# Seventeen opening dummy products, values on 120 partitions, a head planned anew, and a last block summed in two column parts

## The chip, the cores and the metric

The kernel runs on one core of one Trainium2 chip. The metric is the device time of one execution in microseconds (us), taken as the median of several executions. A core has a matrix engine (TensorE, "PE" in the profile; "PEld" is its loading of weights), a vector engine (VectorE, "DVE"), a scalar engine (ScalarE, "ACT"), GpSimd ("POOL") and SyncE ("SP"), whose queue starts nearly all transfers from memory here. Each engine takes its instructions strictly in the order in which they were written, and waits for the others through semaphores.

## What is computed

Two batches of 12480 tokens with 128 channels go through an attention over 49 agents and then through a two-layer MLP with 2048 hidden features and a leaky rectifier. All data are 32-bit floats.

```python
scale = 1.0 / np.sqrt(q.shape[-1])
def sm(a, b):                       # softmax over the last axis
    s = scale * (a @ b.transpose(0, 2, 1))
    e = np.exp(s - s.max(-1, keepdims=True))
    return e / (e.sum(-1, keepdims=True) + 1e-09)
agent_v = sm(agents, k) @ v         # (2, 49, 128): over all 12480 tokens
x = sm(q, agents) @ agent_v         # (2, 12480, 128)
h = x.reshape(-1, 128) @ w_in       # (24960, 2048)
out = np.maximum(0.01 * h, h) @ w_out
```

## The kernel before

The program has a head, a body and a tail.

**The head** needs all of batch 0's keys and values, because `agent_v` sums over every token. Keys come in 13 chunks (`load_k`, 480 KB each), values in 13 chunks (`load_v`), weights in 8 pieces (`load_w`; they arrive as 64-bit floats, 512 KB a piece, and are turned into 32-bit floats by hand) and the first queries in `load_q`. The host lays the values out as 120 partitions for each batch; for batch 0 `load_v` joins both batches' partitions and takes the first 128 of them, so that 8 rows of batch 1 come along unused. The loads of the head stand on SP's queue in the order of the string `ORDER` (k, v, w and q, one letter for a load). Keys and values share a ring of `LD = 9` buffers, weights one of `NVR = 4`: a load waits until the one 9 (or 4) places before it in its ring has been used up.

What the engines do with the loads: `k_score` (TensorE, the line `ps[r, j * w:j * w + NA]`, L397 before) gives a chunk's scores. For the first `NW = 4` chunks a weight load covers 120 columns, later ones go as 64 and 56 columns. `k_run` (VectorE, L417) keeps the running maximum, `k_copy` (ScalarE) stores the scores. When all 13 chunks are through, `k_max0` to `k_max3` (from L431 on) reduce the maximum, `k_sub` and `k_exp` make the exponentials, and `k_av32` (L541) sums exponentials times values, chunk after chunk, into one accumulator. Then `f_copy`, `f_tr`, `f_avT` and `m_half` form the folded weights `m_hi` and `m_lo`, with which the body's first product (`mm1`, tile `h`, L825) can start. Meanwhile each weight piece is converted: `conv_bits` (L273, L274), `conv_mant`, `conv_exp`, `conv_low` (L289), `conv_sign` (L296), `conv_mul` (L303), and `wo_hi_of`, `wo_lo_of` (L309) for pieces of `w_out`. The first two blocks of queries run through their softmax in the head too (`chain`).

The order of all this on each engine is made by a small planner, the class `Plan`. It keeps a time at which each engine is free, takes the step that can begin first, and adds to each step's beginning a number of `slack` by which it may be put off (the table `slack`, and `other` for the query chain). A TensorE gap in the plan is filled with dummy products (`heat`, L1015: 128 by 128 from a tile of zeros, each recorded as two matmuls). Ahead of the plan stands `heat(9, True)`, the opening dummy products.

**The body** goes over 52 blocks (`NBLK`) of 480 tokens (`NB`), 8 steps (`NP`) each. A step has six pairs of matmuls for the first layer (`mm1`), the rectifier split into two parts (`relu`: `hi` on ScalarE, `lo` on VectorE), and, two steps later, six pairs for the second layer (`mm2`, L855). Each pair works on both halves of the 128 rows (`ROWS`), 64 rows each, into two PSUM banks; `o_copy` and `o_add` add the two and store the block. The PSUM pairs `turns[0]` and `turns[1]` change roles from block to block: one is the block's output, the other (`aux2`) serves side work.

**The tail** is the last block's `o_copy`: for each half of 240 tokens ScalarE copies one bank (L883), VectorE adds the other (L884), and a transfer stores the half, the first from SP's queue, the second from ScalarE's.

Of the kernel before, what the change touches and what calls it, by code (L numbers as in the profile page):

```python
# [13 lines left out]
ALU = mybir.AluOpType  # L14
# [4 lines left out]
class Plan:  # L19
# [6 lines left out]
    def add(self, name, eng, cost, fn, args, after, lag=80):  # L26
        self.steps[name] = eng, cost, fn, args, after, lag
# [47 lines left out]
def tile_agent_attention_then_leaky_mlp(  # L75
# [27 lines left out]
    nc = tc.nc  # L103
# [3 lines left out]
    P = 128  # L107
    TP = 120
    NJ = N // TP
    G = 4  # L110
    NB = G * TP
    BPB = N // NB
    NBLK = B * BPB
    NF = DFF // P
# [12 lines left out]
    NP = NF // 2  # L127
# [3 lines left out]
    RP = 4  # L131


    ORDER = "kqwkkkwwkkkkwqkkkkkwvwvvvvvvvvvvwvvwq"
    HOP = 90
    WW = slice(2 * C, 3 * C)
    EW = HALF + NA
# [21 lines left out]
    def aux2():  # L159
        return turns[owner[0] % 2]  # L160
# [4 lines left out]
    def halves(i):  # L165

        owner[0] = i
        return [turns[(i + 1) % 2][:, g, :] for g in range(2)]
# [9 lines left out]
    ROWS = slice(0, HALF), slice(HALF, P)  # L178
# [10 lines left out]
    wo_hi = const.tile([P, NF, C], F32R, name="wo_hi")  # L189
    wo_lo = const.tile([P, NF, C], F32R, name="wo_lo")  # L190
# [6 lines left out]
    l_hi = [const.tile([P, C], F32R, name=f"l_hi{b}") for b in range(B)]  # L197
    l_lo = [const.tile([P, C], F32R, name=f"l_lo{b}") for b in range(B)]
# [4 lines left out]
    run = const.tile([TP, CH, NA], F32, name="run")  # L203
# [13 lines left out]
    def load_v(b, c):  # L217

        t = ld.tile([P, CH, C + 2], F32, tag="ld", name="vt")
        j = slice(c * CH, (c + 1) * CH)  # L220
        if b == 0:
            nc.sync.dma_start(out=t, in_=v.rearrange("b p j c -> (b p) j c")[:P, j, :])
        else:
            nc.sync.dma_start(out=t[:TP], in_=v[b, :, j, :])
        v_t[b, c] = t

    def load_q(i):
# [146 lines left out]
    def prep_parts(b):  # L374
        a, t = a_sb[:, b, :], prep_t.pop(b)
        for o, x, n in SLOTS[:2] + ((SL + A0 - 1, A0 - 1, 1),):
            nc.vector.tensor_copy(t[:, o:o + n], a[:, x:x + n])
        nc.vector.tensor_copy(a_hl[b][:, :HALF], t)
        sub(nc.vector, a_hl[b][:, HALF:], t, a_hl[b][:, :HALF].bitcast(F32))
# [277 lines left out]
    qs_t, s_t, x_t, r_t2, pT_t = {}, {}, {}, {}, {}  # L657
# [158 lines left out]
    h_t, r_t, o_t = {}, {}, {}  # L816
# [28 lines left out]
    def mm2(i, p):  # L845

        b = i // BPB
        if p == 0:
            o_t[i] = halves(i)
        o = o_t[i]  # L850
        hi, lo = r_t.pop((i, p))

        def add(w, x, start=False, stop=False):
            for g, r in enumerate(ROWS):
                nc.tensor.matmul(o[g][:, :NB], lhsT=w[r], rhs=x[r], start=start, stop=stop)  # L855

        for g in range(2):
            f = 2 * p + g
            add(wo_hi[:, f, :], hi[:, g], start=(f == 0))
            add(wo_lo[:, f, :], hi[:, g])  # L860
        if p == (NP // 2 if i % BPB else NP - 1):
            t = pT_t[i]
            for w, x, g in ((l_hi, 0, 0), (l_lo, 0, 1), (l_hi, 1, 0)):
                g ^= i % 2 == 0
                r = ROWS[g]
                nc.tensor.matmul(  # L866
                    o[g][:, :NB], lhsT=w[b][r], rhs=t[r, x], start=False, stop=False
                )
        for g in range(2):
            f = 2 * p + g  # L870
            add(wo_hi[:, f, :], lo[:, g], stop=(f == NF - 1))

    def o_copy(i):
        t = p1.tile([P, 2, NB], F32, tag="oT", name="oT")
        o = o_t.pop(i)
        if i < NBLK - 1:
            for g in range(2):
                nc.scalar.copy(t[:, g], o[g][:, :NB])  # L878
            x_t["o"] = t
            return  # L880
        h = NB // 2
        for c, eng in ((slice(0, h), nc.sync), (slice(h, NB), nc.scalar)):
            nc.scalar.copy(t[:, 1, c], o[1][:, c])  # L883
            nc.vector.tensor_tensor(out=t[:, 0, c], in0=o[0][:, c], in1=t[:, 1, c], op=ALU.add)  # L884
            eng.dma_start(out=out[:, i * NB + c.start:i * NB + c.stop], in_=t[:, 0, c])

    def o_add(i):
# [7 lines left out]
    def at(step, fn, *a):  # L895
# [3 lines left out]
    chain = (  # L899
        (-16, q_hi), (-16, q_lo), (-13, q_mm), (-13, q_turn), (-12, q_mm2), (-12, q_x), (-12, q_add),  # L900
        (-11, q_tr), (-10, q_red), (-10, q_swap), (-9, q_mx), (-9, q_sub), (-7, q_exp),
        (-7, q_sum), (-7, q_swap), (-6, q_rec), (-6, q_norm), (-5, p_trans), (-4, p_hi),
        (-4, p_lo), (-4, p_dup),
    )
# [37 lines left out]
    for b in range(1, B):  # L942
# [21 lines left out]
        for h in range(NH):  # L964
            s = n0 + h * NP // 2
            if h % 2 == 0:
                c = h // 2
                at(s - 5, load_v, b, c)
                at(s, k_sub, b, c, nc.gpsimd)
                at(s + 2, k_exp, b, c)  # L970
            at(s + 3, k_ehi, b, h, h, nc.scalar)
            at(s + 3, k_elo, b, h, h, nc.gpsimd)
            at(s + 1, k_vhi, b, h, h, nc.vector)
            at(s + 2, k_vlo, b, h, h, nc.gpsimd)
            if h % 2:
                at(s + lag, k_av2, b, h // 2)
# [11 lines left out]
    with tc.manual_schedule():  # L988
        nc.sync.dma_start(out=a_sb, in_=agents)
        loads = [(x, ORDER[:i].count(x)) for i, x in enumerate(ORDER)]  # L990
        nc.vector.memset(pre[:, 0, :], 0.0)
# [7 lines left out]
        for o, a, n in SLOTS:  # L999
            nc.gpsimd.tensor_tensor(  # L1000
                out=sel[:, o:o + n], in0=ident[:EW, a:a + n],
                in1=ident[:EW, HALF + a:HALF + a + n], op=ALU.add,
            )
        nc.gpsimd.tensor_tensor(
            out=less, in0=ident[:EW, :NA + 1], in1=ident[:EW, HALF:EW + 1], op=ALU.add
# [6 lines left out]
        def heat(n, start=False):  # L1012

            for i in range(n):
                nc.tensor.matmul(  # L1015
                    avw[1][:, :C] if closed else avw[1][:, WW], lhsT=pre[:, 0, :P],
                    rhs=pre[:, 0, :C], start=bool(closed) or start and i == 0,
                    stop=bool(closed),
                )

        plan = Plan(HOP, {
            "pe": 5300, "dve": 4700, "act": 3000, "pool": 8000, "sp": 700, "dma": 3300,
        })
        heat(9, True)
        prep_parts(0)

        add = plan.add
        dve, act = nc.vector, nc.scalar
        fetch = {
            "k": (lambda c: load_k(0, c), 1210),  # L1030
            "v": (lambda n: load_v(0, TURN[n]), 1280),
            "w": (load_w, 1250), "q": (load_q, 610),
        }
        ring, held = [], {"k": ("run",), "w": ("low", "sign"), "v": ("vdone",)}
        sent, come = [], []
        for what, c in loads:
# [4 lines left out]
            elif what != "q":  # L1041
                if len(ring) >= LD:
                    x, n = ring[-LD]
# [18 lines left out]
        for n in range(w7):  # L1062
            r = [("mul", n - RP)] if n >= RP else []
# [17 lines left out]
        for i in range(2):  # L1081
            last = ("q", i)
            for n, (_, fn) in enumerate(chain[:7 if i == 0 else -1]):
                eng, cost = costs[fn]
# [30 lines left out]
        for n in range(NCH):  # L1115
            for g in range(2):
                h = 2 * n + g
# [24 lines left out]
        for (_, a), (b, _) in zip(users, users[1:]):  # L1142
            plan.steps[b][4].append(a)
        slack = {
            "tr": 300, "wmm": 1200, "wohi": 600, "wolo": 800, "bits": 100, "exp": 600,
            "low": 800, "sign": 800, "mul": 400, "sub": 200, "e": 200, "av": 300,
            "wcopy": 300, "run": 400,
        }
        for name in plan.steps:
            if isinstance(name, tuple):  # L1150
                other = (0, 100)[name[1]] if name[0] == "chain" else 0
                plan.wait[name] = slack.get(name[0], other)
        with tc.tile_pool(name="ps_s", bufs=4, space=PSUM) as pools["s"]:
            end = f_tr, f_den, ("mm", 0), ("mm", 0.5), "go"
# [3 lines left out]
        for s in range(len(steps) + LAG):  # L1158
            if s < len(steps):
                i, f = steps[s]  # L1160
                mm1(i, f)
                if f == LAG:
                    owner[0] = i
                    if i > 0:
                        o_copy(i - 1)
                relu(i, f)
                for fn, a in side.get(s, ()):
                    fn(*a)
            if s >= LAG:
                mm2(*steps[s - LAG])  # L1170
        o_copy(NBLK - 1)


# [37 lines left out]
```

## Time and profile before

| what | value |
|---|---|
| time before, median of 3 runs | 959.97 us (958.66 to 961.91) |
| the profiled execution's own time | 965.88 us |
| span of the profiled execution, first to last instruction | 964.1 us |
| TensorE busy, share of the span | 953.6 us, 99% |
| VectorE, ScalarE, GpSimd busy | 77%, 64%, 39% |
| read and written in memory | 43.22 MB, 12.78 MB |

The span is what the profiler saw between the first and the last instruction; the execution's own time lies 1.8 us above it. Busy time on TensorE counts every stretch in which a matmul is under way, whether it runs fast or slowly, so 99% does not say that TensorE is at its peak.

### The profile page before, as it was taken

The numbers are of one execution on the slowest core, as the hardware profiler recorded it, in microseconds if no ns is written. First come the engines' busy times: TensorE is split into PE (matmuls) and PEld (weight loads), VectorE is DVE, ScalarE is ACT, GpSimd is POOL, SyncE is SP. The second block draws the span as 40 slices with busy tenths as digits, with TensorE's granted clock in tenths as the row PEclk, the third lists the DMA queues.
The fourth block names the chain that finished last, engine by engine and source line by source line (L and its number), as shares of the span: only waits on it lengthen the run. The fifth ranks groups of instructions, "written<-read, shape, count | busy, mean of one in ns | idle before, by whom it ended". The sixth has DMA issues, their size and how long they took to land.

```text
span 964.1 us, 22835 instructions
## 1 busy us (share of the span) xinstructions
PE 953.6 (99%) x9404; PEld 879.7 (91%) x9404; DVE 737.8 (77%) x1068; ACT 613.4 (64%) x907; POOL 375.4 (39%) x548
## 2 busy tenths in 40 slices
PE   9999999999999999999999999999999999999998
PEld 9867888888888988988888899999999999999997
DVE  4877767777888888888877777777777777777774
ACT  3775566656666676666666666666666666666654
POOL 1002243334557566566443433334343334343420
PEclk9999999999999999999999999999999999999999
DMA  9850422212322312322111121211111121212110
GB/s 349 314 172 11 125 83 83 86 60 63 79 68 63 94 52 74 84 64 73 33 46 47 32 62 32 53 42 47 48 42 52 43 52 42 52 40 54 34 41 22
DMA packets 28867, 70.25 MB, mean 73 GB/s; under 512 B 4419, under 2 KB 17859, under 8 KB 28763
## 3 DMA queue, kind: packets, MB, share of 16 engines
q1 hardware_dynamic: 28619, 68.67, 23.7%
q8 instruction: 74, 1.21, 0.5%
q14 instruction: 30, 0.25, 0.1%
q10 hardware_dynamic: 144, 0.12, 0.0%
HBM read 43.22 MB, written 12.78 MB: 58 GB/s over the span
## 4 chain that ended last, share of the span: by engine, by line
PE 95%; DVE 3%; ACT 1%; issue 1%; DVEq 0%; ACTq 0%
PE turn L855 57%; PE h L825 28%; PE turn L690 2%; PE turn L866 2%; PE sc L397 1%; PE turn L397 1%; PE turn L509 1%; PE turn L1015 1%; DVE run L417 0%; DVE lo L839 0%; DVE s_sb L469 0%; ACT hi L838 0%; PE turn L541 0%; DVE w_out_sb L303 0%; PE turn L613 0%
## 5 line engine op out<-in xcount | busy, mean ns | idle before, releaser
L839 DVE SCALAR_TENSOR_TENSOR lo<-h,hi 128x960 fp32r<-128x960 f32 x416 | 478.9, 1151 | 192.0 <-ACT hi L838 191.1
L838 ACT ACTIVATE hi<-h 128x960 fp32r<-128x960 f32 x416 | 405.9, 976 | 291.9 <-PE h L825 267.3
L855 PE MATMUL turn<-hi,wo_hi 64*128 64x480 f32 x1664 | 421.3, 380 | 0.0
L855 PE MATMUL turn<-hi,wo_lo 64*128 64x480 f32 x1664 | 417.9, 376 | 0.0
L825 PE MATMUL h<-pT,m_hi 64*128 64x480 f32 x1664 | 342.1, 377 | 0.1
L855 PE MATMUL turn<-lo,wo_hi 64*128 64x480 f32 x1664 | 341.4, 375 | 0.0
L855 PEld LDWEIGHTS turn<-hi,wo_lo 64*128 64x128 f32 x1664 | 257.6, 184 | 11.0
L855 PEld LDWEIGHTS turn<-hi,wo_hi 64*128 64x128 f32 x1664 | 253.9, 184 | 13.3 <-issue 2.2
L855 PEld LDWEIGHTS turn<-lo,wo_hi 64*128 64x128 f32 x1664 | 236.1, 184 | 12.8
L825 PEld LDWEIGHTS h<-pT,m_hi 64*128 64x128 f32 x1664 | 234.9, 184 | 13.9 <-issue 0.8
L825 PE MATMUL h<-pT,m_lo 64*128 64x480 f32 x832 | 242.7, 376 | 0.0
L825 PEld LDWEIGHTS h<-pT,m_lo 64*128 64x128 f32 x832 | 136.8, 184 | 7.0 <-DVE m_lo L638 0.2
L362 POOL TENSOR_TENSOR qlo<-qt,qhi 128x480 fp32r<-128x480 f32 x50 | 61.4, 1228 | 81.2 <-PE turn L613 66.8
L362 POOL TENSOR_TENSOR pT<-pt,pT 64x480 fp32r<-64x480 f32 x50 | 61.1, 1222 | 60.2 <-ACT pT L790 60.2
L733 POOL COPY mx<-mx 32x15 f32<-32x15 f32 x50 | 9.5, 190 | 186.6 <-DVE mx L726 182.4
L362 POOL TENSOR_TENSOR d<-st,mm 64x375 f32<-64x375 f32 x50 | 41.4, 829 | 93.0 <-DVE mm L739 93.0
L889 POOL TENSOR_TENSOR oT<-oT 128x480 f32<-128x480 f32 x51 | 62.5, 1225 | 12.8 <-issue 10.0
L878 ACT COPY oT<-turn 128x480 f32<-128x480 f32 x102 | 52.0, 562 | 1.1 <-PE turn L855 1.1
L776 POOL TENSOR_TENSOR pd<-d,rs 64x375 f32<-64x375 f32 x50 | 41.0, 819 | 28.8 <-DVE rs L771 28.8
L690 PE MATMUL turn<-qhi,a_hl 64*128 64x240 f32 x208 | 47.4, 279 | 0.5 <-DVE m_lo L638 0.5
L733 POOL COPY sm<-sm 32x15 f32<-32x15 f32 x50 | 9.5, 190 | 97.3 <-DVE sm L756 97.3
L690 PE MATMUL turn<-qlo,a_hl 64*128 64x240 f32 x208 | 46.9, 274 | 0.0
(159 smaller groups left out, 921.6 us busy)
## 6 DMA issues: line engine op xcount, KB each, us to landing
kt<-in_k_dram SPq DMA_DIRECT2D x26, 480.0 KB, 5.6
qt<-in_q_dram SPq DMA_DIRECT2D x52, 240.0 KB, 2.9
pT<-pT SPq DMA_DIRECT2D x102, 120.0 KB, 2.3
out_dram<-oT SPq DMA_DIRECT2D x51, 240.0 KB, 2.0
vt<-in_v_dram SPq DMA_DIRECT2D x13, 520.0 KB, 7.5
vt<-in_v_dram SPq DMA_DIRECT2D x13, 487.5 KB, 4.5
w<-in_w_in_dram SPq DMA_DIRECT2D x4, 512.0 KB, 6.3
w<-in_w_out_dram SPq DMA_DIRECT2D x4, 512.0 KB, 8.5
```

Of the source, the lines that this page charges most:

```text
L362: eng.tensor_tensor(out=o, in0=x, in1=y, op=ALU.subtract)
L397: nc.tensor.matmul(ps[r, j * w:j * w + NA], lhsT=k_t[b, c][:, j, r], rhs=a_sb[:, b, :], start=j == 0 or not late(b, c), stop=True, skip_gr ...
L690: nc.tensor.matmul(s_t[i][:, m, :h], lhsT=a_hl[i // BPB][r], rhs=x[r, m * h:(m + 1) * h], start=(s == 0 and n == 0), stop=(n == 1), skip_g ...
L733: by(i).tensor_copy(r[x, :, 1], r[y, :, 0])
L776: by(i).tensor_tensor(out=pd[:n, :, :A0], in0=d[:n], in1=w[:n].to_broadcast([n, NT, A0]), op=ALU.mult,)
L825: nc.tensor.matmul(ps[:, g, :NB], lhsT=w[b][r, cols(2 * p + g)], rhs=t[r, x], start=(n == 0), stop=(n == 2),)
L838: nc.scalar.activation(hi, ps, AF.Relu)
L839: nc.vector.scalar_tensor_tensor(out=lo, in0=ps, scalar=0.0, in1=hi.bitcast(F32), op0=ALU.max, op1=ALU.subtract,)
L855: nc.tensor.matmul(o[g][:, :NB], lhsT=w[r], rhs=x[r], start=start, stop=stop)
L866: nc.tensor.matmul(o[g][:, :NB], lhsT=w[b][r], rhs=t[r, x], start=False, stop=False)
L878: nc.scalar.copy(t[:, g], o[g][:, :NB])
L889: nc.gpsimd.tensor_tensor(out=t[:, 0], in0=t[:, 0], in1=t[:, 1], op=ALU.add)
```

## The change

The opening dummy products go from 9 to 17, and the planner's TensorE starts at 6700 instead of 5300 (nanoseconds). Batch 0's values are loaded on the 120 partitions that are used, as batch 1's are. `ORDER` and the planner's slacks are new. In the last block every product of `mm2` is done in two column parts, 320 tokens into the one PSUM pair and 160 into the other, and `o_copy` stores these two parts in place of two halves.

```diff
-    ORDER = "kqwkkkwwkkkkwqkkkkkwvwvvvvvvvvvvwvvwq"
+    ORDER = "kwqkwkkwkkwkkqkwkkkkvvvvvvvvvwvvwvvwq"
...
-        if b == 0:
-            nc.sync.dma_start(out=t, in_=v.rearrange("b p j c -> (b p) j c")[:P, j, :])
-        else:
-            nc.sync.dma_start(out=t[:TP], in_=v[b, :, j, :])
+        nc.sync.dma_start(out=t[:TP], in_=v[b, :, j, :])
...
         if p == 0:
-            o_t[i] = halves(i)
-        o = o_t[i]
+            o_t[i] = parts(i)
         hi, lo = r_t.pop((i, p))
+        for c, o in o_t[i]:
+            w = c.stop - c.start
...
+            for g in range(2):
+                f = 2 * p + g
+                add(wo_hi[:, f, :], hi[:, g], start=(f == 0))
+                add(wo_lo[:, f, :], hi[:, g])
...
+    def parts(i):
+
+        o = halves(i)
+        if i < NBLK - 1:
+            return [(slice(0, NB), o)]
+        h = 2 * NB // 3
+        return [(slice(0, h), o), (slice(h, NB), [aux2()[:, g, :] for g in range(2)])]
...
-        h = NB // 2
-        for c, eng in ((slice(0, h), nc.sync), (slice(h, NB), nc.scalar)):
-            nc.scalar.copy(t[:, 1, c], o[1][:, c])
-            nc.vector.tensor_tensor(out=t[:, 0, c], in0=o[0][:, c], in1=t[:, 1, c], op=ALU.add)
+        for (c, o), eng in zip(o_t.pop(i), (nc.sync, nc.scalar)):
+            w = c.stop - c.start
...
+            nc.scalar.copy(t[:, 1, c], o[1][:, :w])
+            nc.vector.tensor_tensor(out=t[:, 0, c], in0=o[0][:, :w], in1=t[:, 1, c], op=ALU.add)
             eng.dma_start(out=out[:, i * NB + c.start:i * NB + c.stop], in_=t[:, 0, c])
...
-            "pe": 5300, "dve": 4700, "act": 3000, "pool": 8000, "sp": 700, "dma": 3300,
+            "pe": 6700, "dve": 4700, "act": 3000, "pool": 8000, "sp": 700, "dma": 3300,
         })
-        heat(9, True)
+        heat(17, True)
...
-            "tr": 300, "wmm": 1200, "wohi": 600, "wolo": 800, "bits": 100, "exp": 600,
+            "tr": 200, "wmm": 300, "wohi": 2000, "wolo": 800, "bits": 600, "mant": 300,
```

Where TensorE's work stands at the start of the program, before (first fence) and in the changed kernel (second). `pre` is the dummy tile, `sc<-a_sb,kt` a chunk's scores on 120-column weights (8 matmuls a chunk), `qhi` and `qlo` are queries, L533 and L530 clear the accumulator.

```order
L1015 MATMUL turn_79<-pre 128x128 x9
L397 MATMUL sc<-a_sb,kt 120x49 x8
L690 MATMUL turn_80<-qhi,a_hl_94 128x240 x2
L690 MATMUL turn_80<-qlo,a_hl_94 128x240 x2
L533 MATMUL turn_79<-pre 128x130
L1015 MATMUL turn_79<-pre 128x128 x2
L690 MATMUL turn_80<-qhi,a_hl_94 128x240 x2
L690 MATMUL turn_80<-qlo,a_hl_94 128x240 x2
L1015 MATMUL turn_79<-pre 128x128 x2
L397 MATMUL sc<-a_sb,kt 120x49 x24
```

```order
L1022 MATMUL turn_79<-pre 128x128 x17
L394 MATMUL sc<-a_sb,kt 120x49 x8
L530 MATMUL turn_79<-pre 128x130
L394 MATMUL sc<-a_sb,kt 120x49 x8
L687 MATMUL turn_80<-qhi,a_hl_94 128x240 x2
L687 MATMUL turn_80<-qlo,a_hl_94 128x240 x2
L1022 MATMUL turn_79<-pre 128x128 x2
L394 MATMUL sc<-a_sb,kt 120x49 x8
L1022 MATMUL turn_79<-pre 128x128 x2
L394 MATMUL sc<-a_sb,kt 120x49 x8
```

The second chunk's scores now stand directly behind the first's, ahead of the queries' products; before, two query products (8 matmuls), the clearing and two groups of dummies stood between them, and the second, third and fourth chunk followed in one run.

The loads on SP's queue, before (first fence) and now (second). `kt` is a key chunk, `vt` a value chunk, `w` a weight piece, `qt` a block of queries; the size is partitions by 32-bit words.

```order
L214 DMA kt<-in_k_dram 128x960
L230 DMA qt<-in_q_dram 128x480
L240 DMA w_157<-in_w_in_dram 128x1024
L214 DMA kt<-in_k_dram 128x960 x3
L245 DMA w_165<-in_w_out_dram 128x1024
...
L214 DMA kt<-in_k_dram 128x960 x5
L240 DMA w_281<-in_w_in_dram 128x1024
L222 DMA vt<-in_v_dram 128x1040
L245 DMA w_412<-in_w_out_dram 128x1024
L222 DMA vt<-in_v_dram 128x1040 x10
L240 DMA w_609<-in_w_in_dram 128x1024
L222 DMA vt<-in_v_dram 128x1040 x2
```

```order
L214 DMA kt<-in_k_dram 128x960
L237 DMA w_163<-in_w_in_dram 128x1024
L227 DMA qt<-in_q_dram 128x480
L214 DMA kt<-in_k_dram 128x960
L242 DMA w_169<-in_w_out_dram 128x1024
...
L237 DMA w_225<-in_w_in_dram 128x1024
L214 DMA kt<-in_k_dram 128x960 x4
L221 DMA vt<-in_v_dram 120x1040 x9
L242 DMA w_552<-in_w_out_dram 128x1024
L221 DMA vt<-in_v_dram 120x1040 x2
L237 DMA w_616<-in_w_in_dram 128x1024
L221 DMA vt<-in_v_dram 120x1040 x2
```

Weight pieces stand earlier among the keys. The sixth piece (`w_412` before, `w_552` now) has moved from behind the first value chunk to behind the ninth. Ahead of the first value chunk stand the agents, 13 key chunks, 5 weight pieces and 2 blocks of queries in both; ahead of the last one 7 weight pieces in both.

The end of TensorE's program, its last step of `mm2`, before (first fence) and now (second). `turn_79` and `turn_80` are the two PSUM pairs.

```order
L855 MATMUL turn_79<-hi,wo_hi 128x480 x2
L855 MATMUL turn_79<-hi,wo_lo 128x480 x2
L855 MATMUL turn_79<-hi,wo_hi 128x480 x2
L855 MATMUL turn_79<-hi,wo_lo 128x480 x2
L855 MATMUL turn_79<-lo,wo_hi 128x480 x4
```

```order
L853 MATMUL turn_79<-hi,wo_hi 128x320 x2
L853 MATMUL turn_79<-hi,wo_lo 128x320 x2
L853 MATMUL turn_79<-hi,wo_hi 128x320 x2
L853 MATMUL turn_79<-hi,wo_lo 128x320 x2
L853 MATMUL turn_79<-lo,wo_hi 128x320 x4
L853 MATMUL turn_80<-hi,wo_hi 128x160 x2
L853 MATMUL turn_80<-hi,wo_lo 128x160 x2
L853 MATMUL turn_80<-hi,wo_hi 128x160 x2
L853 MATMUL turn_80<-hi,wo_lo 128x160 x2
L853 MATMUL turn_80<-lo,wo_hi 128x160 x4
```

Each pair of 480 columns has become one of 320 and one of 160 with the same weights, loaded twice. In the whole last block 99 matmuls become 198.

## Rows read from the trace of the kernel before

**Rows 1.** Windows of core 0 by stage: busy us and count per engine, PEclk, DMA, GB/s.

```profile
0.00:60.44 60.44, 56.19 (x686) 51.93 (x686) 43.36 (x102) 35.07 (x65) 2.78 (x15) 1.00 0.86 313
...
100.00:940.00 840.00, 840.00 (x8191) 780.64 (x8191) 654.71 (x917) 543.43 (x794) 364.15 (x522) 1.00 0.21 58
959.60:964.10 4.50, 0.00 (x0) 0.00 (x0) 0.82 (x2) 0.72 (x2) 0.00 (x0) 0.91 0.17 55
```

**Rows 2.** Windows inside the head, same columns: PE, PEld, DVE, ACT, POOL.

```profile
10.00:25.00 15.00, 15.00 (x76) 14.56 (x76) 6.87 (x13) 6.55 (x13) 0.00 (x0) 1.00 1.03 413
25.00:38.67 13.67, 13.67 (x329) 12.85 (x328) 12.01 (x24) 9.55 (x19) 0.00 (x0) 1.00 0.73 244
38.67:60.44 21.77, 18.97 (x246) 16.26 (x244) 20.57 (x52) 16.58 (x32) 0.00 (x0) 1.00 0.86 314
```

**Rows 3.** Timeline of PE: three groups of dummy products, start and us.

```profile
1.45 4.21 PE L1015 MATMUL turn<-pre 128*128 128x128 f32 x18 [1.45 <-DVE pre L991]
...
23.05 2.26 PE L1015 MATMUL turn<-pre 128*128 128x128 f32 x12
...
29.59 1.06 PE L1015 MATMUL turn<-pre 128*128 128x128 f32 x8
```

**Rows 4.** Windows of the key scores alone (L397) on PE.

```profile
12.69:22.17 9.48, 9.48 (x48) 1.00 1.03 415
25.24:29.10 3.86, 3.86 (x128) 1.00 0.88 297
```

**Rows 5.** Timeline of DVE: start, us, operation, [idle before <-releaser].

```profile
16.01 0.56 DVE L417 TENSOR_TENSOR run<-sc,run 120x392 f32<-120x392 f32 x1 [2.98 <-PE sc L397]
...
38.67 0.82 DVE L431 TENSOR_REDUCE wide<-run 120x49 f32<-120x392 f32 x1
```

**Rows 6.** What SP's queue waited for in 0 to 75 us: total, times, longest.

```profile
SPq L245 <- DVE e L296: 4.7, 1, 4.7
```

**Rows 7.** Transfers issued in 2.5:2.7, 22.7:22.9, 32.3:32.5, 36.4:36.6: size, us to landing.

```profile
kt<-in_k_dram SPq DMA_DIRECT2D x1, 480.0 KB, 6.5
...
w<-in_w_in_dram SPq DMA_DIRECT2D x1, 512.0 KB, 6.3
...
vt<-in_v_dram SPq DMA_DIRECT2D x1, 520.0 KB, 7.0
...
vt<-in_v_dram SPq DMA_DIRECT2D x1, 520.0 KB, 10.4
```

**Rows 8.** Timeline of SP's queue, 31.6:37 and 43:44: second to ninth value chunk, tenth.

```profile
31.90 4.89 SPq L222 DMA_DIRECT2D vt<-in_v_dram  x8
...
43.50 0.33 SPq L222 DMA_DIRECT2D vt<-in_v_dram  x1
```

**Rows 9.** Transfers of values: one issued in 26.4:26.5; batch 1's, from the page.

```profile
vt<-in_v_dram SPq DMA_DIRECT2D x1, 520.0 KB, 3.9
...
vt<-in_v_dram SPq DMA_DIRECT2D x13, 487.5 KB, 4.5
```

**Rows 10.** Timeline of PE at the end of the head: last value chunk, first `mm1`.

```profile
56.45 0.76 PE L541 MATMUL turn<-vt,s_sb 120*49 120x130 f32 x10
...
60.44 0.70 PE L825 MATMUL h<-pT,m_hi 64*128 64x480 f32 x4
```

**Rows 11.** Timeline of PEld, 73.0 to 73.6: weight loads for 240 and 480 columns.

```profile
73.12 0.19 PEld L690 LDWEIGHTS turn<-qlo,a_hl 64*128 64x128 f32 x2
73.23 0.19 PEld L855 LDWEIGHTS turn<-hi,wo_hi 64*128 64x128 f32 x2
73.34 0.19 PEld L855 LDWEIGHTS turn<-hi,wo_lo 64*128 64x128 f32 x2
73.56 0.18 PEld L855 LDWEIGHTS turn<-hi,wo_hi 64*128 64x128 f32 x2
```

**Rows 12.** Timeline of the tail: PE's last matmuls, VectorE's last work.

```profile
959.00 0.60 PE L855 MATMUL turn<-lo,wo_hi 64*128 64x480 f32 x3
...
960.90 0.41 DVE L884 TENSOR_TENSOR oT<-turn,oT 128x240 f32<-128x240 f32 x1 [0.43 <-ACT oT L883]
```

More of the change, by code (lines that the diff above doesn't have):

```diff
@@ L848, in mm2 @@
         if p == 0:
-            o_t[i] = halves(i)
-        o = o_t[i]
+            o_t[i] = parts(i)
         hi, lo = r_t.pop((i, p))
[L853 to L868, printed above, removed]
@@ L869, in mm2, with add @@
-        for g in range(2):
-            f = 2 * p + g
-            add(wo_hi[:, f, :], lo[:, g], stop=(f == NF - 1))
+        for c, o in o_t[i]:
+            w = c.stop - c.start
+            def add(wt, x, start=False, stop=False):
+                for g, r in enumerate(ROWS):
+                    nc.tensor.matmul(
+                        o[g][:, :w], lhsT=wt[r], rhs=x[r, c], start=start, stop=stop
+                    )
+            for g in range(2):
+                f = 2 * p + g
+                add(wo_hi[:, f, :], hi[:, g], start=(f == 0))
+                add(wo_lo[:, f, :], hi[:, g])
+            if p == (NP // 2 if i % BPB else NP - 1):
+                t = pT_t[i]
+                for wt, x, g in ((l_hi, 0, 0), (l_lo, 0, 1), (l_hi, 1, 0)):
+                    g ^= i % 2 == 0
+                    r = ROWS[g]
+                    nc.tensor.matmul(
+                        o[g][:, :w], lhsT=wt[b][r], rhs=t[r, x, c], start=False, stop=False
+                    )
+            for g in range(2):
+                f = 2 * p + g
+                add(wo_hi[:, f, :], lo[:, g], stop=(f == NF - 1))
@@ L873, in o_copy @@
+    def parts(i):
[4 more added lines that the diff above has]
+        return [(slice(0, h), o), (slice(h, NB), [aux2()[:, g, :] for g in range(2)])]
     def o_copy(i):
         t = p1.tile([P, 2, NB], F32, tag="oT", name="oT")
[L875 to L880, printed above, removed]
-        h = NB // 2
@@ L882, in o_copy @@
-        for c, eng in ((slice(0, h), nc.sync), (slice(h, NB), nc.scalar)):
-            nc.scalar.copy(t[:, 1, c], o[1][:, c])
-            nc.vector.tensor_tensor(out=t[:, 0, c], in0=o[0][:, c], in1=t[:, 1, c], op=ALU.add)
+        for (c, o), eng in zip(o_t.pop(i), (nc.sync, nc.scalar)):
+            w = c.stop - c.start
+            if i < NBLK - 1:
+                for g in range(2):
+                    nc.scalar.copy(t[:, g], o[g][:, :w])
+                x_t["o"] = t
+                return
+            nc.scalar.copy(t[:, 1, c], o[1][:, :w])
+            nc.vector.tensor_tensor(out=t[:, 0, c], in0=o[0][:, :w], in1=t[:, 1, c], op=ALU.add)
@@ L1144, in tile_agent_attention_then_leaky_mlp @@
         slack = {
-            "tr": 300, "wmm": 1200, "wohi": 600, "wolo": 800, "bits": 100, "exp": 600,
-            "low": 800, "sign": 800, "mul": 400, "sub": 200, "e": 200, "av": 300,
-            "wcopy": 300, "run": 400,
+            "tr": 200, "wmm": 300, "wohi": 2000, "wolo": 800, "bits": 600, "mant": 300,
+            "exp": 800, "low": 600, "sign": 800, "mul": 600, "sub": 300, "e": 100,
+            "copy": 400, "run": 100, "av": 300,
         }
@@ L1150, in tile_agent_attention_then_leaky_mlp @@
             if isinstance(name, tuple):
-                other = (0, 100)[name[1]] if name[0] == "chain" else 0
+                other = (600, 200)[name[1]] if name[0] == "chain" else 0
                 plan.wait[name] = slack.get(name[0], other)
```

## The prediction

> **What bounds the kernel now.** I read the windows by stage first. From 100 to 940 us TensorE is busy in 840.00 of 840.00 us [rows 1]: the body is one stream of matmuls that the change leaves alone, except in its last block. What the change can move lies in the first 60.44 us, before the first `mm1`, and in the last 4.5.
>
> Inside the head the bound changes. From 10 to 25 us TensorE is busy throughout and VectorE for only 6.87 of 15 us; from 38.67 on VectorE is busy for 20.57 of 21.77, and from 25 to 38.67 the transfers use only 0.73 of their engines [rows 2]. So TensorE holds the start and VectorE, fed late, holds the end. Why TensorE is slow at the start is read from the dummy products, all of one shape: 18 take 4.21 us at 1.45 us (0.23 each), 8 take 1.06 at 29.59 (0.13 each), and the group at 23.05, 12 in 2.26, lies between [rows 3]. [...] Three key chunks of 120-column weights take 9.48 us at the lower level, 3.16 a chunk; four later ones, of 64 and 56 columns and at the upper level, take 3.86, or 0.97 a chunk [rows 4]. VectorE waits for them: 2.98 us ahead of the second running maximum at 16.01, and the reduction over all keys begins only at 38.67 [rows 5].
>
> Lateness on VectorE then holds the loads: the sixth weight piece waited 4.7 us on SP's queue for `conv_sign` of the second piece [rows 6], with all values but the first behind it. The loads themselves keep a steady pace when nothing holds them: a key chunk issued at 2.6 lands at 9.1, the fifth weight piece, issued at 22.8 and sixteen transfers later, lands at 29.1; that is 1.25 us a transfer. Eight value chunks are issued from 31.90 to 36.8; the second, issued at 32.4, lands at 39.4, the eighth, at 36.5, lands at 46.9: 1.25 each again [rows 7, 8].
>
> **The change, part by part.** *Opening.* Before, 9 products (18 matmuls) ran for 4 us at the lower level without a rise, the scores that followed ran without one, and the rise came inside the group of dummies at 23.05 [rows 3]. Now 17 products would take 34 x 0.22 = 7.5 us, to 9.0, if the clock stayed low. I take it that nearly twice as many dummies in one run bring the rise before they end, as that later group did; this is a choice, and a rival below has the other case. The run then ends between 6.5 us (rise at about 4) and 9.0; the first scores, which began at 5.45, begin 1 to 3.5 us later, but a chunk then takes 1.6 us in place of 3.16. Four chunks cost 6.4 us in place of 12.6, so TensorE has the fourth chunk's scores when its keys land (below 14 us, not at 22.17), and from there the keys set the pace.
>
> [...]
>
> *Loads.* Agents, 13 key chunks, 5 weight pieces and 2 blocks of queries stand ahead of the first value chunk in both orders, so they land by 29.1 as before. If nothing holds SP's queue, 13 value chunks and 2 weight pieces follow at 1.25: the last value chunk lands at 29.1 + 15 x 1.25 = 47.9. What could hold it: the sixth weight piece now stands behind nine value chunks, and `conv_sign` of the second piece is long done then. The tenth value chunk needs the first one used up by `k_av32`; before, it was issued at 43.50 [rows 8], 4.8 us behind the reduction over all keys. Now it is to land at 29.1 + 11 x 1.25 = 42.9, so with 3.9 us to land [rows 9] it has to be issued by 39. VectorE had 43.36 - 20.57 = 22.8 us of work ahead of the reduction [rows 1, 2]. The last keys land at about 27.9, so the reduction can begin near 31, and the first value chunk is used up by 36. I book no stall.
>
> *Values on 120 partitions.* The bytes fall from 520 to 487.5 KB, 6%. If time followed bytes, 13 chunks would land 13 x 0.08 = 1.0 us earlier. The rows do not show that: batch 1's loads, on 120 partitions, take 4.5 us to land (with a queries' load beside them), a 128-partition one with an empty queue 3.9 [rows 9]. I take zero, and keep 1.0 as the other end. [...]
>
> *End of the head.* From the last value chunk's products at 56.45 to the first `mm1` at 60.44 are 3.99 us [rows 10]; that chain (copy, transpose, copy, product, scaling) is unchanged. With the last values at 47.9 the first `mm1` begins at 51.9, or 8.6 us earlier. VectorE must keep up: from the reduction on it was busy 20.57 us [rows 2], of which some 2 us of query work now stand ahead of it; from 31 that ends at 49.6, close behind the transfers. The range for this term is 6.5 (VectorE 2 us late) to 10 (values scale with bytes, no gaps).
>
> *Tail.* A pair of 480 columns takes 0.22 us from one weight load to the next, one of 240 columns 0.11 [rows 11]. By columns, 320 and 160 would take 0.146 + 0.073, nothing lost. But no row shows a 64 by 128 weight load sooner than 0.11 behind the one before. If that is a floor, a 160-column pair takes 0.11 and each of the 49.5 pairs of the last block (99 matmuls) loses 0.037, 1.85 us in all. I take the floor, the nearest row. It is TensorE time on the path. At the very end, before, TensorE stopped at 959.60, and the last of two copies and two adds ended at 961.31 [rows 12], 1.71 behind it. Now the 320-token part is complete six 160-column pairs (0.66 us) before TensorE stops: its copy and add (0.41 for 240 tokens [rows 12], taken as 0.43 and 0.5 for 320) run until 0.4 behind the stop, and the short add ends about 0.75 behind it. Gain 0.95. Net: 0.9 later, between 0.95 earlier and 0.9 later.
>
> **The sum.** 965.88 - 8.6 + 0.9 = 958.2 us for the profiled execution. That execution lies 5.9 us above the median of the runs shown, 959.97, and the body can hardly differ between executions. How much of the 5.9 us is the late clock, and how much comes with profiling, the rows don't say. If all of it is the clock, the timed runs had it up earlier, and 958.2 stands as it is; if none, they too lose 7.7 and give 952.3. I take the first: an execution of the kernel before whose clock rises in its opening comes to 965.88 - 8.6 = 957.3 by the same sum, and the fastest timed one, 958.66, is near that.
>
> **The rivals.**
> *The full price.* The timed runs of before were at the lower level until 24 us as the profiled one was; then the median loses 7.7: 952.3 (950 to 954). For it: three runs span only 3.3 us, so none of them alone looks like a rise that the others lack. Against it: the profiled one lies well outside them.
> *The opening costs and gives nothing (slower).* If the clock does not rise before the 17 products are through, the first scores begin at 9.0, not 5.45. The fourth chunk's end: 9.0 + 4 x 3.16, plus clearing 0.6, query products 0.7, four dummies 1.8, is 24.7 against 22.17, and everything to 38.67 hangs on that chain: +2.5, with the tail 963.4. It decides at the second group of scores: if they begin after 12 us, this is the case.
> *VectorE or the plan takes the bound.* The clock rises, but the tenth value chunk is held, or VectorE finishes the weights 2 to 4 us late: 960.2 to 962.2, no measurable change.
> *The replan does nothing of its own.* This one is part of the forecast: at equal clock both orders end on the same transfers, so the gain over a timed run that was already fast is the tail's alone.
>
> **How the numbers follow.** A measurement of this kernel tells about 0.3%, 2.9 us, from no change: faster is below 957.1, slower above 962.9. The forecast, 958.2 with a range of its own from 956 to 960, has 0.55, of which 0.15 lies below 957.1. The full price has 0.25, the late VectorE 0.12, the slower one 0.08. Faster: 0.15 + 0.25 = 0.40; same: 0.40 + 0.12 = 0.52; slower: 0.08. For 8 in 10 the range takes in the full price and most of the late VectorE: 951.5 to 961.5.
>
> **What would show it.** Dummy products at 0.23 and then 0.13 us inside the opening; scores of the second to fourth chunk 1.6 us long; the reduction over keys at 30 to 32; value chunks landing 1.25 apart with the last at 47 to 49; the first `mm1` at 50.5 to 53; 160-column pairs 0.11 apart and the last add 0.8 behind TensorE's end. The prediction is wrong if the scores still take 3.16 us, if SP's queue waits for `k_av32`, or if the fast runs of before already lie where the changed kernel's do and its tail costs more than 2 us.

## The result, and the profile after

The changed kernel takes 973.47 us (median of 6 runs, 971.79 to 974.39), the kernel before in the same sets 959.32 (6 runs, 958.52 to 965.74): a ratio of 1.0133, 95% interval 1.0104 to 1.0162. It is slower, by more than the 0.3% that count, where 958.2 was forecast. Its profiled execution took 973.78 us in a span of 972.0; the first `mm1` begins at 67.11, 6.67 later than before [rows 10] and 15.2 later than predicted.

The windows in the head, with the columns of [rows 2]:

```profile
2.00:10.00 8.00, 8.00 (x58) 7.92 (x56) 3.81 (x10) 2.41 (x5) 1.46 (x6) 1.00 0.94 317
10.00:25.00 15.00, 14.88 (x246) 13.79 (x245) 13.14 (x26) 11.90 (x25) 0.00 (x0) 1.00 1.03 414
25.00:40.00 15.00, 12.03 (x211) 10.78 (x211) 12.39 (x35) 6.90 (x14) 0.00 (x0) 1.00 0.99 265
40.00:62.00 22.00, 15.84 (x161) 12.68 (x158) 11.82 (x23) 11.54 (x19) 0.00 (x0) 0.77 0.98 236
```

Up to 25 us more gets done than before, where TensorE was still at its lower level (0.23 us a dummy matmul, not the 0.13 of its upper one [rows 3]): it issues 246 matmuls between 10 and 25 us in place of 76, and VectorE is busy for 13.14 us in place of 6.87. Then the last two columns part. The transfer engines stay busy at 0.98 to 0.99, but move 265 and then 236 GB/s instead of 414. They are not idle; each transfer takes longer (261 ns for a packet of 4,160 bytes, 161 before).

TensorE's timeline, three stretches, with what ended an idle time behind the arrow:

```profile
1.45 6.14 PE L1022 MATMUL turn<-pre 128*128 128x128 f32 x34 [1.45 <-DVE pre L998]
7.43 1.78 PE L394 MATMUL sc<-a_sb,kt 128*120 128x49 f32 x16
...
14.30 1.78 PE L394 MATMUL sc<-a_sb,kt 128*120 128x49 f32 x16
...
27.85 1.22 PE L394 MATMUL sc<-a_sb,kt 128*64 128x49 f32 x32 [0.62 <-DMA kt<-in_k_dram]
29.89 1.10 PE L394 MATMUL sc<-a_sb,kt 128*64 128x49 f32 x32 [0.82 <-DMA kt<-in_k_dram]
31.82 1.10 PE L394 MATMUL sc<-a_sb,kt 128*64 128x49 f32 x32 [0.83 <-DMA kt<-in_k_dram]
...
45.71 1.09 PE L538 MATMUL turn<-vt,s_sb 120*49 120x130 f32 x16 [0.83 <-DMA vt<-in_v_dram]
47.59 1.09 PE L538 MATMUL turn<-vt,s_sb 120*49 120x130 f32 x16 [0.79 <-DMA vt<-in_v_dram]
50.52 1.98 PE L538 MATMUL turn<-vt,s_sb 120*49 120x130 f32 x16 [1.83 <-DMA vt<-in_v_dram]
...
54.44 1.98 PE L538 MATMUL turn<-vt,s_sb 120*49 120x130 f32 x16 [1.22 <-DMA vt<-in_v_dram]
...
57.93 1.98 PE L538 MATMUL turn<-vt,s_sb 120*49 120x130 f32 x16
...
60.80 1.09 PE L538 MATMUL turn<-vt,s_sb 120*49 120x130 f32 x16
...
63.13 1.09 PE L538 MATMUL turn<-vt,s_sb 120*49 120x130 f32 x16 [0.81 <-DMA vt<-in_v_dram]
...
67.11 0.70 PE L822 MATMUL h<-pT,m_hi 64*128 64x480 f32 x4
```

The last key chunks come some 2 us apart, although they still lie on 128 partitions: they share the engines with the first value loads, which are issued from 21.25 us on. From the one at 43.78 us on the value chunks are used 1.9 to 3.9 us apart, six of the eight directly after a wait for their load. While TensorE waits so, its granted clock falls (0.77 over 40 to 62 us; by the clock records of the trace it is at 0.5, the lower of the two levels recorded, from 50.2 to 60.5), and the 16 products of three chunks take 1.98 us each in place of 1.09. From the last value chunk to the first `mm1` it is 3.98 us, as before [rows 10].

### The profile page after: what moved, and what is told of

Its sections match the earlier page's. It is cut to its first block, busy times and chain, and to the rows that moved or that the text cites. A ratio compares the mean times of both kernels' runs of the same rounds, so it can differ in the third digit from the quotient of the medians.

```text
span 972.0 us, 23046 instructions
## 1 busy us (share of the span) xinstructions
PE 954.1 (98%) x9509; PEld 884.4 (91%) x9509; DVE 738.0 (76%) x1068; ACT 613.4 (63%) x907; POOL 374.6 (39%) x548
## 4 chain that ended last, share of the span: by engine, by line
PE 91%; DMA 6%; DVE 1%; ACT 1%; issue 0%; SPq 0%; ACTq 0%
PE turn L853 57%; PE h L822 27%; DMA vt<-in_v_dram 3%; PE turn L687 2%; PE turn L866 2%; PE turn L394 1%; PE turn L506 1%; DMA kt<-in_k_dram 1%; DMA w<-in_w_out_dram 1%; DMA qt<-in_q_dram 1%; DVE lo L836 0%; ACT hi L835 0%; PE turn L610 0%; DVE m_lo L635 0%; PE turn L613 0%
## 5 line engine op out<-in xcount | busy, mean ns | idle before, releaser
L853 PE MATMUL turn<-hi,wo_hi 64*128 64x480 f32 (+2 forms) x1696 | 423.0, 376 | 0.0
L853 PE MATMUL turn<-hi,wo_lo 64*128 64x480 f32 (+2 forms) x1696 | 419.7, 373 | 0.0
L853 PE MATMUL turn<-lo,wo_hi 64*128 64x480 f32 (+2 forms) x1696 | 342.5, 372 | 0.0
L853 PEld LDWEIGHTS turn<-hi,wo_lo 64*128 64x128 f32 x1696 | 261.9, 184 | 9.8
L853 PEld LDWEIGHTS turn<-hi,wo_hi 64*128 64x128 f32 x1696 | 258.5, 184 | 12.0 <-issue 2.2
L853 PEld LDWEIGHTS turn<-lo,wo_hi 64*128 64x128 f32 x1696 | 238.9, 184 | 11.2
```

What stands on the lines that cost most here:

```text
L853: nc.tensor.matmul(o[g][:, :w], lhsT=wt[r], rhs=x[r, c], start=start, stop=stop)
```

## The experiments

The first theory: a load on 120 partitions is itself slow on the transfer engines. Its rivals: the new order of the loads, the 17 dummies with their clock, the split of the last block.

**The 128 partitions back.** In the changed kernel:

```
-        nc.sync.dma_start(out=t[:TP], in_=v[b, :, j, :])
+        if b == 0:
+            nc.sync.dma_start(out=t, in_=v.rearrange("b p j c -> (b p) j c")[:P, j, :])
+        else:
+            nc.sync.dma_start(out=t[:TP], in_=v[b, :, j, :])
```

> The changed kernel, with the first batch's thirteen value chunks loaded on 128 partitions again; the loads' order, the plan, the 17 dummy products and the last block's split stay. Theory (a load on 120 partitions is itself slower on the transfer engines, about 1.95 us a chunk against 1.25): the value chunks land 1.25 apart again, the first mm1 begins near 52 in place of 67.11, and the time is 957.5 to 960. If the new order of the loads or the plan is the cause, the chunks still land about 1.9 apart and the time stays at 972 to 974. If the dummies or the clock are the cause, likewise 972 to 974. If the last block's split is the cause, the first mm1 does not move and the time stays.

Measured: 959.91 us (12 runs), a ratio to before of 0.9995 (0.9966 to 1.0024). The windows 25 to 40 and 40 to 62, and TensorE's timeline at the last value chunk and the first `mm1`:

```profile
25.00:40.00 15.00, 13.83 (x246) 12.82 (x248) 14.20 (x39) 8.79 (x19) 0.00 (x0) 1.00 1.02 411
40.00:62.00 22.00, 20.62 (x208) 15.07 (x203) 18.31 (x33) 16.77 (x29) 0.00 (x0) 1.00 0.65 234
```

```profile
49.27 1.09 PE L541 MATMUL turn<-vt,s_sb 120*49 120x130 f32 x16 [0.16 <-DMA vt<-in_v_dram]
...
53.27 0.70 PE L825 MATMUL h<-pT,m_hi 64*128 64x480 f32 x4
```

The rate is 411 GB/s again, TensorE hardly waits for values, the clock stays up (1.00 over 40 to 62 us), and the first `mm1` comes 13.84 us earlier. The trace has every packet of a transfer: between 27 and 40 us the values' packets of 4,160 bytes took 161 ns here (median) and 261 in the changed kernel, and the weights' packets of 4,096 bytes beside them took 159 (40 to 48 us) against 266 (40 to 62). This one line carries the whole loss.

**The 120 partitions alone.** The kernel before with only that line of the change (the minus and plus above exchanged).

> The kernel before, with nothing changed but the first batch's value chunks loaded on 120 partitions in place of 128. Theory (120 partitions are slow in any order): from the first value chunk on, 13 chunks at about 1.95 us in place of 1.25 are 9.1 us more, so the last lands near 58 or later and the time is 966 to 974. If only the new order of the loads makes them slow, the time stays at 958.5 to 960; if the slowness needs both, something between.

Measured: 971.41 us (9 runs, 966.27 to 975.39), ratio 1.0104 (1.0072 to 1.0136). Its window from 40 to 62 us in the profile:

```profile
40.00:62.00 22.00, 16.57 (x202) 13.89 (x200) 14.41 (x40) 12.62 (x23) 0.00 (x0) 0.92 0.99 235
```

The same 235 GB/s with the engines full. Its first `mm1`:

```profile
68.81 0.71 PE L822 MATMUL h<-pT,m_hi 64*128 64x480 f32 x4
```

That is 8.37 us later than in the profiled execution before [rows 10]; in both TensorE rises to its upper level late (77 and 76 matmuls between 10 and 25 us, where the changed kernel has 246). The old order with 120 partitions loses too.

**Other cuts of the 120 rows.** The changed kernel, each value chunk as two transfers; in the second kernel 64 stands for 112.

```
-        nc.sync.dma_start(out=t[:TP], in_=v[b, :, j, :])
+        for r in (slice(0, 112), slice(112, TP)) if b == 0 else (slice(0, TP),):
+            nc.sync.dma_start(out=t[r], in_=v[b, r, j, :])
```

> The changed kernel, with each value chunk of the first batch loaded as two transfers, rows 0 to 111 and rows 112 to 119, to the same tile; all else as changed. [...] If every load of fewer than 128 partitions is slow, or the destination's 120 partitions are the cause, the time stays at 970 to 975. The new order, the dummies and the split expect no change from 973.

> The changed kernel, with each value chunk of the first batch loaded as two transfers of 64 and 56 rows; all else as changed. [...] If any load of fewer than 128 partitions is slow, 970 to 975. The other theories expect no change from 973.

Measured: 972.09 us (ratio 1.0103, 1.0068 to 1.0137) and 972.72 (1.0109, 1.0074 to 1.0143); 267 and 269 GB/s from 25 to 40 us, 238 and 243 from 40 to 62. Neither helps. A number of rows that is a multiple of 16 does not bring the rate back by itself. It is the 112 rows that say so; the 64 and 56 could be slow for a reason of their own, as 64 and 64 are below.

**Loads by themselves.** Next, loads that nothing reads were added to the kernel before, in quiet stretches of its body. The first set, with the form of 120 rows as the example:

```
+    def probe_120(b):
+        t = ld.tile([P, CH, C + 2], F32, tag="ld", name="n120")
+        nc.sync.dma_start(out=t[:TP], in_=v[b, :, :CH, :])
...
+        for _ in range(4 if x % 6 < 4 else 1):
+            at(NP * (30 + x) + 5, fn, 0)
```

> The kernel before, with loads added in the body that nothing reads, each form in a block of its own, twice over, while SP's queue is otherwise idle: four loads of 128 rows, four of 120, four of 112, four tiles of 128 rows as 64 and 64, and single loads of 8 long rows (20,384 bytes each) to partitions 0, 4, 8 to 28, and to partitions 0 to 7. [...] The new order plays no part here; its theory expects all forms alike per row. The time itself should stay within 1 us of the kernel before.

Measured, with what else was moved meanwhile counted in: over each train of four tiles 323 and 335 GB/s for 128 rows, 218 and 222 for 120, 255 and 243 for 112, 255 and 234 for 64 and 64. The packets of 4,160 bytes took 161 ns (median) in the loads of 128 rows, 296 and 272 in those of 120, 235 and 220 in those of 112, 272 and 280 as 64 and 64. So 64 and 64 are slow, with 128 partitions, the same bytes and twice as many transfers. The 8 long rows went at 138 GB/s on every fourth partition and at 118 on neighbouring ones. A queries' load ran beside them. The run took 961.89 us, outside the 1 us around the kernel before that was expected; the added loads are not the reason, as is shown further down.

**Where the rows come from.** The same forms, three tiles in a row, on ScalarE's queue, clear of other loads, once with the kernel's source and once with rows end to end:

```
+    pitched = v.rearrange("b p j c -> (b p) j c")[:P, :CH, :]
+    dense = v.rearrange("b p (o j) c -> (b p o) j c", j=CH)[:P]
```

> The kernel before, with loads added in the body that nothing reads, on ScalarE's queue in a quiet stretch of each block: three tiles in a row of 128 rows, of 120 rows, and of 128 rows as 64 and 64, each form once from rows that lie 54,080 bytes apart in memory, as the kernel's value chunks do, and once from rows that lie end to end (4,160 bytes apart); each of the six twice over. If the distance of the rows in memory makes the loads of 120 and of 64 and 64 slow, they go at the rate of 128 (some 400 GB/s) from rows end to end, and at 240 to 260 from rows far apart. If what they write makes them slow, both sources give 240 to 260 against 400. If a long train of loads is needed for it, all go alike here, which the first of these measurements speaks against.

Measured (966.11 us; windows over each train of the first round, in the order end to end 128, 120, 64 and 64, then far apart):

```profile
606.90:612.20 5.30, 5.30 (x52) 5.30 (x50) 3.80 (x5) 4.08 (x7) 2.04 (x2) 1.00 0.78 297
623.20:630.20 7.00, 7.00 (x70) 7.00 (x68) 4.88 (x6) 5.02 (x8) 3.50 (x5) 1.00 0.85 209
640.10:647.10 7.00, 5.84 (x53) 5.14 (x51) 3.50 (x5) 4.42 (x7) 2.34 (x4) 1.00 0.92 222
657.70:662.60 4.90, 4.90 (x48) 4.77 (x46) 3.44 (x5) 3.63 (x6) 2.04 (x2) 1.00 0.87 319
674.00:681.00 7.00, 7.00 (x70) 7.00 (x68) 4.89 (x6) 4.96 (x8) 3.44 (x5) 1.00 0.89 213
690.90:697.70 6.80, 5.86 (x54) 5.18 (x52) 3.51 (x5) 4.44 (x7) 2.36 (x4) 1.00 0.93 229
```

The last column is the one to read: 297 and 319 for 128 rows, 209 to 229 for the rest, whichever the source; all lie below the sizes expected. How far apart the rows lie in memory is out; three tiles are enough to show it. What is left of the theories here is what the loads write. That is an argument by what was ruled out; no run shows how it would slow them.

**Which partitions are written.** Single loads of long rows, alike in bytes within 8 and within 16 rows, one form of the first set as the example (the second set has them on ScalarE's queue):

```
+    def probe_8_step4():
+        nc.sync.dma_start(out=s_flat[0:32:4], in_=v_row[:8])
```

> The kernel before, with single loads of long rows (20,384 bytes each) added in the body that nothing reads, some 4 us behind the queries' load of their block, each form in a block of its own and twice over: 8 rows on neighbouring partitions, on every second, fourth and eighth one, then 16 rows on neighbouring partitions and on every fourth. [...] Rival (the partitions written do not matter): all forms take the same time a row, and 16 rows as long as 8. [...]

> As the measurement before, single loads of long rows (20,384 bytes each) that nothing reads, each form in a block of its own and twice over, but issued on ScalarE's queue some 4 us later in the block, so that no queries' load runs beside them. Forms: 4 rows on neighbouring partitions; 8 rows on neighbouring, on every fourth and on every eighth partition; 15 rows on every eighth; 16 rows on neighbouring, on every second and on every fourth. [...] Rival (the partitions written do not matter): all 0.8 to 1.0.

In the first of these (961.82 us) the queries' load still ran beside them, since both waited on SP's queue: 16 rows on neighbouring partitions went at 132 GB/s, on every fourth at 190, the queries' bytes counted in. From the first packet's start to the last one's end, 8 rows took 2.9 and 2.1 us on neighbouring partitions, 1.8 and 1.5 on every second, 1.7 and 1.7 on every fourth, 1.8 and 1.9 on every eighth. In the second set, clear of that load (965.94 us), 4 rows on neighbouring partitions went at 45 and 33 GB/s. The other forms, windows over each load of the second round, in the order 8 rows on neighbouring, every fourth and every eighth partition, 15 on every eighth, 16 on neighbouring, every second and every fourth:

```profile
760.30:762.60 2.30, 2.30 (x26) 2.07 (x24) 1.56 (x3) 1.38 (x3) 0.86 (x2) 1.00 0.36 71
777.40:778.90 1.50, 1.50 (x16) 1.46 (x14) 0.84 (x3) 1.08 (x2) 0.65 (x1) 1.00 0.40 109
793.70:795.30 1.60, 1.60 (x18) 1.60 (x17) 0.93 (x3) 1.14 (x2) 0.73 (x1) 1.00 0.38 102
810.40:812.50 2.10, 2.10 (x24) 2.10 (x22) 1.44 (x3) 1.45 (x2) 1.09 (x2) 1.00 0.59 146
826.10:829.00 2.90, 2.90 (x30) 2.90 (x29) 2.17 (x3) 1.48 (x3) 1.27 (x3) 1.00 0.63 112
843.10:845.00 1.90, 1.90 (x21) 1.90 (x19) 1.24 (x3) 1.39 (x2) 0.83 (x1) 1.00 0.62 172
859.40:861.20 1.80, 1.80 (x20) 1.80 (x19) 1.13 (x3) 1.25 (x2) 0.82 (x1) 1.00 0.66 186
```

Neighbouring partitions give 71 GB/s for 8 rows and 112 for 16, spread ones 102 to 109 and 172 to 186. So which partitions are written matters, by a factor of about 1.5 in these single loads of 1.5 to 2.9 us. The rival, all forms alike at 0.8 to 1.0 us, is out. Among the spread forms none is ahead in both rounds: 8 rows on every fourth and every eighth partition went at 109 and 102 GB/s (86 and 109 in the first round), 16 on every second and every fourth at 172 and 186 (209 and 130). A gap is left: which rows are in flight at one moment in a load of 120 was not seen, so whether they are neighbours there is not shown.

Of the added loads with rows of 4,160 bytes only the one of 128 partitions in one piece has the higher rate: 297 to 335 GB/s in the windows above, against 209 to 255 for the others.

**Dummies and last block.** Three kernels separate the rest: the first with 9 dummies again, the second with the last block in one piece again, the third being the kernel before with 17 dummies.

```
-        heat(17, True)
+        heat(9, True)
```

```
-        if i < NBLK - 1:
-            return [(slice(0, NB), o)]
-        h = 2 * NB // 3
-        return [(slice(0, h), o), (slice(h, NB), [aux2()[:, g, :] for g in range(2)])]
+        return [(slice(0, NB), o)]
```

```
-        heat(9, True)
+        heat(17, True)
```

> The changed kernel with the first batch's values on 128 partitions and 9 opening dummy products in place of 17. If the 17 products are what brings the clock up early, this one has runs near 966 more often than the one with 17 (3 of 12 there), as the kernel before has, and others near 959 to 960; its fastest runs stay at 959.5. If the dummies do not matter, its runs spread as with 17.

> The changed kernel with the first batch's values on 128 partitions and the last block summed in one piece as before. If the split costs by the floor under weight loads, 0.9 to 1.2 us less than with the split: most runs at 958.4 to 959.0. If the split is free or gains, 959.6 to 961.

> The kernel before with 17 opening dummy products in place of 9, nothing else. If the early clock is all that the opening brings, most runs lie at 958.3 to 959 and fewer near 966 than in the kernel before (5 of 20 there). If the 8 more products cost their 1.8 to 3.5 us, the fastest runs lie at 960 or above.

Measured: 967.74 us for the first (4 runs, 967.58 to 968.56; ratio 1.0094, 1.0081 to 1.0107), none at the 959 to 960 that was expected for some; 961.84 for the second (12 runs; 1.0023, 0.9997 to 1.0049), six at 958.35 to 959.37 and six at 964.31 to 966.28; 959.21 for the third (11 runs, 958.61 to 960.52; 0.9993, 0.9973 to 1.0013). The kernel before, timed 43 times beside the first four experiments and beside these, lay 24 times at 958.3 to 958.9, 9 times at 960.7 to 962.4 and 10 times at 965.8 to 967.4. What the levels are, the traces show. With 9 dummies, on 128 partitions (967.58 us), TensorE's timeline:

```profile
1.45 4.21 PE L1025 MATMUL turn<-pre 128*128 128x128 f32 x18 [1.45 <-DVE pre L1001]
5.45 3.29 PE L397 MATMUL sc<-a_sb,kt 128*120 128x49 f32 x16
```

And the kernel before with the first set of added loads, whose head is that of before (961.89 us):

```profile
1.45 3.99 PE L1048 MATMUL turn<-pre 128*128 128x128 f32 x18 [1.45 <-DVE pre L1024]
5.28 1.78 PE L424 MATMUL sc<-a_sb,kt 128*120 128x49 f32 x16
```

One and the same set of 9 dummies is followed by scores of 3.29 us in the one run and of 1.78 in the other; the run at 965.94 us, whose head is that of before as well, has 3.29 again. The trace's records of the granted clock begin with TensorE's rise to its upper level, and so give its moment: 24.63 us in the profiled execution before (965.88 us) and 24.65 in the run at 965.94, but 5.07, 5.93 and 5.89 in the other three with added loads, all with 9 dummies. So the kernel alone does not settle the rise with 9. In all six traces with 17 it comes at 5.85 to 7.55 us. With an early rise the first `mm1` of the old order begins at 53.29 (the run with the two sources), with a late one at 60.44.

The middle level is an early rise with a fall behind it. In the run at 961.89 the clock rises at 5.07, TensorE idles for 2.26 us ahead of its scores at 28.84, and the granted clock is at the lower level from 28.97 to 32.38 (0.89 over 25 to 40 us). The scores and the window:

```profile
28.84 3.96 PE L424 MATMUL sc<-a_sb,kt 128*64 128x49 f32 x76 [2.26 <-issue]
```

```profile
25.00:40.00 15.00, 11.73 (x192) 10.87 (x192) 10.84 (x27) 6.33 (x14) 0.00 (x0) 0.89 1.00 402
```

Its first `mm1` begins at 56.32, and behind that 903.6 us of span remain, as in the kernel before, so the added loads cost nothing there.

A late rise leaves no mark in the granted clock, since the profile shows 1.00 where it has no record yet (up to 24.63 us in the profiled execution before); a later fall does (0.89 in the window above). The ten executions of the kernel before at 965.8 to 967.4 have a mean granted clock of 0.999 to 1.000. The six at 964.31 to 966.28 of the second kernel here, and the three at 965.94 to 966.98 of the changed one on 128 partitions, have 0.990 to 0.993. Of the four with 9 dummies three have 1.000 and one 0.989. So those nine with 17 look like later falls, not like late rises; no trace of them was kept.

The split of the last block shows best behind the first `mm1`, where the moment of the rise no longer matters. With the split, 958.1 - 53.27 = 904.8 us of span remain (on 128 partitions) and 972.0 - 67.11 = 904.9 (as changed); without, 957.2 - 53.53 = 903.7, as in the kernel before, 964.1 - 60.44 = 903.7. It costs 1.1 to 1.2 us; the low groups of the two kernels with 17 dummies on 128 partitions, at 959.81 and 958.80 on average, lie 1.0 apart.

## Why the prediction was wrong, by its steps

*Values on 120 partitions* is the step that failed. It priced the narrower loads at zero, with 1.0 us of gain as the other end, and kept no end on the side of a loss. The row it chose, 4.5 us for batch 1's load on 120 partitions against 3.9 [rows 9], was put down to a queries' load beside it; it may have held part of the answer, and should have been kept as the other end of the range. By the runs the step costs 13.84 us to the first `mm1` (67.11 - 53.27): 13 value chunks and what is loaded beside them at 236 to 265 GB/s in place of 411 to 414, and TensorE's clock lost while it waits.

With the first `mm1` and the tail as measured, the sum closes: 965.88 - (60.44 - 53.27) + 1.2 = 959.9 us for the kernel on 128 partitions, which took 959.91 in the median, and 965.88 + 6.67 + 1.2 = 973.75 for the changed one, whose profiled execution took 973.78. That shows that nothing else moved, and not that the other terms were right: on 128 partitions the head gains 7.17 us, where 8.6 was booked.

*Opening:* right in kind. The clock rose inside the 34 dummy matmuls (6.14 us, at 5.85), and a chunk of scores took 1.78 us, where 1.6 was said. The 1.6 is half of 3.16, and no run shows that a chunk's time halves: with 9 dummies it took 3.29 us at the lower level and 1.78 at the upper. The fourth chunk was through at 16.1, not below 14; the dummies and query products between the chunks had been left out. The choice that 17 products bring the rise is borne out by all six traces with 17. That the old order can have it with 9 as well, as three traces do, this step did not consider, though the sum's choice rests on it.

*Loads:* on 128 partitions the last value chunk was there at 49.3 us, in place of 47.9, and SP's queue did wait 3.2 us for a `k_av32` there, where no stall was booked, but the tenth chunk went out at 36.65, ahead of the 39 that was asked for, and the transfers ran on at 411 GB/s. *End of the head:* the chain from the last values to the first `mm1` was 3.98 and 4.00 us against 3.99; the first `mm1` on 128 partitions came at 53.27, where 50.5 to 53 was given.

*Tail:* 0.9 later predicted, 1.1 to 1.2 measured. The timeline's last adds of the changed kernel end 0.7 us behind TensorE's last product, as the step has it. The size is off on the side of TensorE: from the first `mm1` to its last product it takes 901.32 us (968.43 - 67.11) in place of 899.16 (959.60 - 60.44 [rows 10, 12]), 2.16 more, where 1.85 was booked:

```profile
968.03 0.40 PE L853 MATMUL turn<-lo,wo_hi 64*128 64x160 f32 x3
968.35 0.78 DVE L891 TENSOR_TENSOR oT<-turn,oT 128x320 f32<-128x320 f32 x2 [2.32 <-ACT oT L890]
```

*The sum's choice*, that the 5.9 us between the profiled execution and the median are the late clock, was right: the kernel before has runs at 958.3 and at 965.8, its head ends at 53.29 with an early rise and at 60.44 with a late one, and no kernel here came near the 952.3 of the full price. The slower rival did not keep to that choice: its 963.4 is summed from the median, 959.97, and from the profiled execution it would be 965.88 + 2.5 + 0.9 = 969.3. The rival "the replan does nothing of its own" holds too: with 17 dummies and the last block whole, the new order has its first `mm1` at 53.53, the old one at 54.21, and their lowest times are 958.35 and 958.61; with 9 dummies and an early rise the old order has it at 53.29.

Open stay why exactly the 120-row load is slow, which is put down to the side that writes only because the other theories fell, why 9 dummies bring the early rise in some runs and not in others, and what sets off the later falls of the clock that the times of the new order point to (3 of 12 runs with the split and 6 of 12 without, on 128 partitions with 17 dummies). No version here is measurably faster than the kernel before.

## What to carry to other kernels

An edit that only makes a load narrower needs a price on both sides of zero (here zero was booked, and it cost 13.84 us to the first `mm1`): look for the rate of such a load in the trace (bytes a second while the engines are full), and where it shows none back to back, keep the loss as an end of the range. A stretch with the transfer engines full and the rate low points to the form of the transfer before its place in the queue, as it did here: the 8 rows of padding that nobody reads are worth 13.6 us (973.47 against 959.91). A granted clock of 1.00 at the start of a profile does not say that TensorE was at its upper level: ahead of the trace's first record of the clock the profile here read 1.00 at either level, and the length of like matmuls told them apart (a chunk's scores took 3.29 and 1.78 us). A profiled execution far from the median may be another level of the same kernel, and the sum has to say against which it is made.

## What the runs showed of the hardware

Not expected: loads on 120 partitions moved 235 to 265 GB/s in the head with the engines 98 to 99% busy, on 128 partitions 411 to 414. 128 rows as 64 and 64 went at 222 and 229 GB/s, the same rows in one load at 297 and 319. Slow value loads also slowed the 128-partition key and weight loads beside them (a weight packet took 266 ns, not 159; a key packet 254 from 27 to 40 us, not 149 as ahead of 25 us). Single loads of 8 and 16 rows to neighbouring partitions went at 71 and 112 GB/s, to spread ones at 102 to 109 and 172 to 186 (65 and 109, and 86 to 109 and 130 to 209, in the first round). And a late transfer cost TensorE twice: its 16 products behind a wait of 1.83 us took 1.98 us, not 1.09.
